# Score matmuls one key unit at a time, and output projections in four column groups

## The chip, the cores and the metric

The kernel runs on one core of one Trainium2 chip. A core has five engines with their own instruction streams: TensorE (PE in the profile, with its weight loads listed apart as PEld), VectorE (DVE), ScalarE (ACT), GpSimd (POOL) and SyncE (SP), which here does nothing but issue DMAs. Sixteen DMA engines move data between the device memory and the core's on-chip memory, SBUF. TensorE writes its results into PSUM, eight banks of 128 partitions by 512 fp32 values. The metric is the device time of one execution in microseconds, as a median of several runs.

## The reference

It is one decode step: a gated sum of an attention block (A) and a gated MLP (B), both fed by the same single row `x` of 1024 values.

```
g = sigmoid((x * gate_w).sum(-1))
q = x @ wq                              # 32 heads of 128
scores = q . k_cache * 128 ** -0.5      # 4 key heads, 65536 keys each; 8 query heads share one key head
p = softmax(scores); o = p . v_cache
a = o.reshape(4096) @ wo                # 4096 x 1024
z = gelu(x @ w_in)                      # 1024 x 3584, two halves z1 and z2
b = (z1 * (w_sp * layernorm(z2) + b_sp)) @ w_out    # 1792 x 1024
out = g * a + (1 - g) * b
```

Almost all of the data is the key and value cache: 2 x 4 x 65536 x 128 in bf16, 134 MB. The weights add 28 MB. Every byte is used once.

## The kernel before, in words

**The stream of loads.** All large inputs pass through a ring of five SBUF slots of 32 KB per partition (4 MB in all per slot). The list `stream` fixes the order: two loads of `wq`, then key pairs with the MLP's weights (`w_in`, `w_out`) in between, then key pairs and value pairs in turn, at the end value pairs alone, and last `wo` in six loads of 2, 2, 2, 1, 0.5 and 0.5 MB. A load of keys or values covers two units of 8192 rows, 4 MB. SP issues load number n (line 358) as soon as everything that reads load n - 5, the one before it in the same slot, is through. `use` and `done` place these issues in the program.

**A key unit.** One unit holds 64 keys on each of the 128 partitions. `k_piece` works on a quarter of it: DVE transposes 128 x 2048 bf16 as 32x32 blocks of fp32 words into a buffer `kt` (line 476), and TensorE multiplies it by the query (line 486). The query stands in `qpad`, a zero-padded buffer: for each of the four `fe` and each quarter j a 128 x 128 window of it is the stationary operand, and a 128 x 512 view of the transposed keys is the moving one. The 16 products of a unit add up in one PSUM bank, so that the scores of 8 heads and 16 groups of keys fill all 128 partitions. `score_piece` (line 499) then copies the bank to SBUF with a running maximum. In the kernel before, two units are treated together: in quarter j both are transposed, and each window of `qpad` is loaded once (the matmul at line 486) and used a second time by a matmul without a weight load (`again`, which the profile lists under line 247). A pair of units therefore takes two PSUM banks and two `kt` buffers at a time, and there are four of each (`SCB`, `NKTS`).

**Softmax and values.** After the eight units of a head, `max_piece` finds the maximum. ACT takes the exponentials (line 516), DVE transposes them (line 521), and TensorE multiplies them with the values (line 530): 16 matmuls of 512 columns, four at a time in four column groups of 32, into bank OB. Values lag keys by nine units. After the last unit of a head, `out_piece` normalises and brings the 1024 outputs of the head into `ovec` (lines 540 to 561).

**Output projections.** `wout_piece` forms the MLP's output row, and the loop at the end forms the attention's. Both take a column of 128 values as weights (one column wide) and stream rows of `w_out` or `wo`. In the kernel before, `project` writes one row of 1024 into partition 0 of two banks, 512 columns each, with one weight load for the two matmuls (lines 619 and 247). `keep` then moves this row to the four partitions 0, 32, 64 and 96 of `brow`, 256 values each: for the MLP by copies (line 638), for the first three parts of `wo` by additions (line 640). The last part of `wo` (heads 24 to 31, three loads) is done in another form (line 685): four column groups of 256 columns, one per quarter of the row, after a clearing of the bank (line 677). Line 691 adds `brow`, and line 694 writes the result.

**Order.** The kernel is a list of recorded operations. `Recorder.plan` derives semaphore waits from what each reads and writes, and each engine runs its own operations in recorded order.

Of the kernel before, what the change touches and what calls it, by code (L numbers as in the profile page):

```python
# [6 lines left out]
F32 = mybir.dt.float32  # L7
ACTF = mybir.ActivationFunctionType
ALU = mybir.AluOpType
# [128 lines left out]
def bass_gated_mix__gqa_block_cached__mixer_gmlp__decode_kernel(  # L138
# [19 lines left out]
    DO = A_wo.shape[1]  # L158
# [8 lines left out]
    NS = 5  # L167
    SLOT = 16384
    QP = 152
    NKTS = 4  # L170
    NSC = 8
    QW = DO // 4
    SCALE = 1.0 / math.sqrt(Dh)
    GELU_C = 0.044715
# [29 lines left out]
    def vw(base, off, dims, p0=0, np_=128):  # L204
        ps = base.ap[0][0]
        return bass.AP(tensor=base.tensor, offset=base.offset + off + p0 * ps,
                       ap=[[ps, np_]] + [list(d) for d in dims])
# [5 lines left out]
    qpad = [ab("QPAD", 4 * QP, 4 * QP * i) for i in range(2)]  # L213
# [3 lines left out]
    yb, ovec, orow, brow = ab("YB", FC), ab("OV", OC), ab("OROW", QW), af("BROW", QW)  # L217
# [14 lines left out]
    ktb = lambda i: ab("KT", 2048, (i % NKTS) * 2048)  # L232
# [3 lines left out]

    bank = [nc.alloc_psum_tensor("pb%d" % i, [128, 512], F32) for i in range(8)]
    FB, PTB, OB, MB = 0, 5, 6, 7
    WB0, WB1 = 0, 7
    SCB = [1, 2, 3, 4]  # L240
    pf = lambda i: bank[i][:, :]
    pbf = lambda i: bank[i][:, :].bitcast(BF16)

    def again(e, prev, out, rhs, start, stop):

        m = prev.ins
        return e.add_instruction(mybir.InstMatmult(  # L247
            start_tensor_calc=start, stop_tensor_calc=stop, tile_size=m.tile_size, tile_position=m.tile_position,
            bass_skip_group_check=True, ldweights=False, name=nc.get_next_instruction_name(), engine=e.engine,
            ins=[e.lower_ap(rhs), list(m.ins)[1]], outs=[e.lower_ap(out)]))  # L250

    R = Recorder()
    P = R.op

    def B(i):
        return ("bank", i)
# [7 lines left out]
        P("POOL", lambda e, i=i: e.memset(qpad[i], 0.0), w=[("qpad", i)])  # L264
    P("DVE", lambda e: e.memset(ones, 1.0), w=["ones"])
    P("DVE", lambda e: e.memset(oneb, 1.0), w=["oneb"])
    P("DVE", lambda e: e.memset(brow, 0.0), w=[("brow", q) for q in range(4)])
    P("DVE", lambda e: e.memset(pf(MB), 0.0), w=[B(MB)])
    P("DVE", lambda e: e.memset(pf(OB), 0.0), w=[B(OB)])
    P("DVE", lambda e: e.memset(pf(FB), 0.0), w=[B(FB)])  # L270
# [59 lines left out]
    for n in range(NU, total + NU + 1):  # L330
        k = n if n < total else None
# [9 lines left out]
    WO = [(0, 0, 8), (1, 0, 8), (2, 0, 8), (3, 0, 4), (3, 4, 6), (3, 6, 8)]  # L341
# [21 lines left out]
    def use(key):  # L363
        n, i = place[key]
        issue(n + 1)
        used.add(key)
        w = WIDTH[key[0]]
        return slot(n)[:, i * w:(i + 1) * w], ("slot", n % NS)

    def done(key):  # L370

        n = place[key][0]
        if key == stream[n][0][-1]:
            issue(n + NS + 1)
# [10 lines left out]
      r=["m32"], w=["sel"])  # L385
# [5 lines left out]
    for fe in range(4):  # L391
        P("DVE", lambda e, fe=fe: e.tensor_copy(vw(sele, 128 * fe, [[32, 4], [1, 32]]),
                                                vw(idb, 64 * (fe // 2) + fe % 2, [[0, 4], [2, 32]])),
          r=["idb"], w=[KSE])


    def f(e):
        for c in range(4):
            ins = e.transpose(pbf(PTB)[:, 2 * c:2 * c + 2], vw(xrow, c, [[4, 128]], 0, 2), idb[0:2, 0:2])
        return ins  # L400
    P("PE", f, r=[KX, "idb"], w=[B(PTB)])
    P("DVE", lambda e: e.tensor_copy(vw(xT, 0, [[4, 2], [1, 4]]), vw(pbf(PTB), 0, [[1, 2], [2, 4]])),
      w=["xT", B(PTB)])
    P("DVE", lambda e: e.tensor_copy(vw(xw, 1, [[3, KC]]), xT), r=["xT"], w=["xw"])
    P("PE", lambda e: e.matmul(pf(MB)[:, 0:2], oneb[0:1, :], wb[0:1, :], start=True, stop=True),  # L405
      r=["oneb", "wsp", "bsp"], w=[B(MB)])
# [6 lines left out]
      r=["ones", "gs"], w=[B(PTB)])  # L413
# [46 lines left out]
    def q_piece(g):  # L460
        for pb in range(4):
            P("DVE", lambda e, pb=pb: e.tensor_copy(vw(qpad[g % 2], 24 + 32 * pb, [[QP, 4], [1, 8]], 32 * pb, 32),
                                                    vw(qall, 8 * g, [[32, 4], [1, 8]], 32 * pb, 32)),
              r=["qall"], w=[("qpad", g % 2)])

    def k_piece(n, j):

        g, u = KV[n]
        if u == 0 and j == 0:
            q_piece(g)  # L470
        i = nbatch[0]
        nbatch[0] += 2
        sb = [SCB[n % 4], SCB[n % 4 + 1]]
        for m in range(2):
            sl, key = use(("k", n + m))
            P("DVE", lambda e, m=m, sl=sl: e.transpose(ktb(i + m).bitcast(F32),  # L476
                                                       sl[:, 2048 * j:2048 * (j + 1)].bitcast(F32)),
              r=[key], w=[("kt", (i + m) % NKTS)])

        def f(e):  # L480
            for fe in range(4):
                f2, ev = fe // 2, fe % 2
                o = QP * fe + 24 - 8 * j
                rhs = [vw(ktb(i + m), 64 * f2 + ev, [[128, 16], [2, 32]]) for m in range(2)]
                st, sp = j == 0 and fe == 0, j == 3 and fe == 3
                ins = e.matmul(pf(sb[0]), qpad[g % 2][:, o:o + 128], rhs[0], start=st, stop=sp)  # L486
                ins = again(e, ins, pf(sb[1]), rhs[1], st, sp)
            return ins
        P("PE", f, r=[("qpad", g % 2), ("kt", i % NKTS), ("kt", (i + 1) % NKTS)], w=[B(sb[0]), B(sb[1])])
        while pend:  # L490
            score_piece(pend.pop(0))
        if j == 3:
            done(("k", n + 1))
            pend.extend([n, n + 1])

    def score_piece(n):
        g, u = KV[n]
        sb = SCB[n % 4]
        P("DVE", lambda e: e.tensor_scalar(scs(n), pf(sb), 0.0, None, op0=ALU.add, op1=ALU.max,  # L499
                                           accum_out=maxc[:, n:n + 1]), w=[("sc", n % NSC), ("mx", n), B(sb)])  # L500
        if u == NU - 1:
            max_piece(g)
# [108 lines left out]
        P("DVE", lambda e: e.scalar_tensor_tensor(yb, z2[:, 0:FC], col(C_OMG), h1, op0=ALU.mult, op1=ALU.mult),  # L611
          r=["z2", "omg", "zg"], w=["yb"])

    def project(e, vec, sl, first, last):

        n = vec.shape[1]
        for c in range(n):
            st, sp = first and c == 0, last and c == n - 1
            ins = e.matmul(pf(WB0)[0:1, :], vec[:, c:c + 1], sl[:, DO * c:DO * c + 512], start=st, stop=sp,  # L619
                           skip_group_check=True)  # L620
            ins = again(e, ins, pf(WB1)[0:1, :], sl[:, DO * c + 512:DO * (c + 1)], st, sp)
        return ins

    def wout_piece(i):
        sl, key = use(("wout", i))
        P("PE", lambda e: project(e, yb[:, 7 * i:7 * (i + 1)], sl, i == 0, i == 1), r=["yb", key], w=[B(WB0), B(WB1)])
        done(("wout", i))
        if i == 1:
            keep(True)

    def keep(first):

        for q in range(4):
            src = pf((WB0, WB1)[q // 2])[0:1, QW * (q % 2):QW * (q % 2 + 1)]
            dst = brow[32 * q:32 * q + 1, :]
            k = [B((WB0, WB1)[q // 2])]
            if first:
                P("DVE", lambda e, dst=dst, src=src: e.tensor_copy(dst, src), w=[("brow", q)] + k)  # L638
            else:
                P("DVE", lambda e, dst=dst, src=src: e.tensor_tensor(dst, src, dst, ALU.add), r=[("brow", q)],  # L640
                  w=[("brow", q)] + k)


    started = set()
# [5 lines left out]

    for si, (k, v, aux) in enumerate(steps):
        nxt = steps[si + 1][1] if si + 1 < len(steps) else None
        while k is None and pend:
            score_piece(pend.pop(0))
        if v is not None and v not in started:
            start_exp(v)
        for j in range(4):
            if k is not None and j % 2 == 0:
                k_piece(k - k % 2, 2 * (k % 2) + j // 2)
            if j == 1 and v is not None:  # L660
                pt_piece(v)
            if j == 2 and nxt is not None:
                start_exp(nxt)
            if j == 3 and v is not None:
                pv_piece(v)
        for a in aux:
            (win_piece if a[0] == "win" else wout_piece)(a[1])


    for i in range(3):  # L670
        sl, key = use(("wo", i, 0))
        P("PE", lambda e, i=i, sl=sl: project(e, ovec[:, 8 * i:8 * (i + 1)], sl, i == 0, i == 2), r=[("ovec", i), key],
          w=[B(WB0), B(WB1)])
        done(("wo", i, 0))
    keep(False)
    FB = SCB[0]
    P("DVE", lambda e: e.memset(pf(FB), 0.0), w=[B(FB)])
    for i, c0, c1 in WO[3:]:
        sl, key = use(("wo", i, c0))

        def f(e, i=i, sl=sl, c0=c0, c1=c1):
            for c in range(c0, c1):
                for q in range(4):
                    o = DO * (c - c0) + QW * q
                    ins = e.matmul(pf(FB)[32 * q:32 * q + 1, 0:QW], ovec[:, 8 * i + c:8 * i + c + 1],  # L685
                                   sl[:, o:o + QW], start=(c == 0), stop=(c == 7),
                                   tile_position=(0, 32 * q), skip_group_check=True)
            return ins
        P("PE", f, r=[("ovec", i), key], w=[B(FB)])
        done(("wo", i, c0))  # L690
    P("DVE", lambda e: e.tensor_tensor(orow[0:97, :], pf(FB)[0:97, 0:QW], brow[0:97, :], ALU.add),
      r=[("brow", q) for q in range(4)], w=["orow", B(FB)])
    osrc = bass.AP(tensor=arena, offset=OFF["OROW"], ap=[[32 * NA, 4], [1, QW]])
    P("SP", lambda e: e.dma_start(out[0, 0].rearrange("(q n) -> q n", n=QW), osrc), r=["orow"], w=["out"], dma="out")

# [29 lines left out]
```

## Time and profile before

| what | value |
|---|---|
| median of 3 runs | 388.36 us (387.95 to 389.19) |
| the profiled execution's own time | 387.95 us |
| its span, first to last instruction | 386.2 us |
| mean granted TensorE clock | 0.80 of full |
| TensorE busy, matmuls | 237.5 us, 62% |
| TensorE busy, weight loads | 66.8 us, 17% |
| VectorE busy | 214.6 us, 56% |
| read from device memory | 162.01 MB, 420 GB/s over the span |

The span and the time differ by 1.75 us, which lie outside the instructions of the engines. Busy times of several engines overlap, so their sum says nothing; what counts is what the engine or the transfer that ended last was waiting for. "PEclk" or "granted clock" is the share of full TensorE speed. Window rows give, for a stretch of the span, each engine's busy time, the granted clock, the mean busy share of the sixteen DMA engines and their rate.

### The profile page before, as it was taken

To read this page: it belongs to the slowest core of one execution; us is meant where nothing else is said; L and a number is where in the kernel's file an instruction comes from. 1 tells how busy PE (TensorE), PEld (TensorE's weight loads), DVE (VectorE), ACT (ScalarE), POOL (GpSimd) and SP (SyncE) were. 2 spreads that over 40 slices of the span, in tenths; PEclk is the share of its full clock that TensorE was granted. 3 is DMA by queue.
4 is the path that set the end of the run, shared out by engine and by line. 5 is a ranking of instruction groups with operands and counts; after the bars stand their busy time and mean duration, and the time that the engine had idled before them with its cause. 6 is when DMAs were issued, how large, how long until landed. Compare 5 with 4: busy or idle time off the path is not lost.

```text
span 386.2 us, 3169 instructions
## 1 busy us (share of the span) xinstructions
PE 237.5 (62%) x1471; PEld 66.8 (17%) x1177; DVE 214.6 (56%) x338; ACT 30.0 (8%) x70; POOL 2.1 (1%) x9
## 2 busy tenths in 40 slices
PE   0443979477587766563668584735774838533394
PEld 0110444411111111011111110101110101211111
DVE  4115464397379983845389747554976557521102
ACT  1000000300002100000001000001010000320000
POOL 2000000000000000000000000000000000000000
PEclk9995869559968999695669786968896958665589
DMA  8999999999999999999999999999999999999992
GB/s 330 434 434 438 426 432 433 433 434 434 434 434 431 433 424 428 431 423 434 431 431 428 433 431 434 429 434 432 434 434 433 431 425 431 436 417 428 421 419 105
DMA packets 6226, 162.21 MB, mean 420 GB/s; under 512 B 700, under 2 KB 708, under 8 KB 964
## 3 DMA queue, kind: packets, MB, share of 16 engines
q1 hardware_dynamic: 6200, 162.01, 97.8%
q8 instruction: 10, 0.16, 0.2%
q14 instruction: 4, 0.03, 0.0%
q10 hardware_dynamic: 12, 0.00, 0.0%
HBM read 162.01 MB, written 0.00 MB: 420 GB/s over the span
## 4 chain that ended last, share of the span: by engine, by line
DMA 62%; PE 19%; DVE 17%; issue 1%; SPq 0%; DVEq 0%
DMA arena<-in_A_k_cache_dram 53%; DVE arena L476 13%; DMA arena<-in_A_v_cache_dram 10%; PE pb L247 7%; PE pb L486 5%; PE pb L619 2%; PE pb L530 2%; PE pb L572 2%; DVE arena L499 2%; DVE arena L521 1%; DVE arena L640 0%; DVE arena L638 0%; DVE arena L547 0%; PE pb L685 0%; PE pb L552 0%
## 5 line engine op out<-in xcount | busy, mean ns | idle before, releaser
L476 DVE STREAM_TRANSPOSE arena<-arena 128x1024 f32<-128x1024 f32 x128 | 149.1, 1212 | 67.2 <-DMA arena<-in_A_k_cache_dram 60.9
L486 PE MATMUL pb<-arena 128*128 128x512 bf16 x256 | 116.9, 456 | 95.5 <-DVE arena L476 88.8
L247 PE MATMUL pb<-arena 128*128 128x512 bf16 (+1 forms) x294 | 131.5, 447 | 0.0
L486 PEld LDWEIGHTS pb<-arena 128*128 128x128 bf16 x256 | 27.9, 109 | 208.1 <-DVE arena L476 123.0
L530 PE MATMUL pb<-arena 128*32 128x512 bf16 x512 | 39.7, 446 | 19.1 <-DMA arena<-in_A_v_cache_dram 16.6
L516 ACT ACTIVATE arena<-arena 128x512 bf16<-128x512 f32 x32 | 23.0, 719 | 245.0 <-DVE arena L521 153.3
L521 DVE STREAM_TRANSPOSE arena<-arena 128x512 bf16<-128x512 bf16 x32 | 22.1, 692 | 17.0 <-PE pb L530 17.0
L499 DVE TENSOR_SCALAR_CACHE_REDUCE arena<-pb 128x512 f32<-128x512 f32 x32 | 20.4, 672 | 2.5 <-PE pb L247 2.5
L530 PEld LDWEIGHTS pb<-arena 128*32 128x32 bf16 x512 | 13.0, 108 | 49.7 <-issue 41.8
L619 PE MATMUL pb<-arena 128*1 128x512 bf16 x38 | 15.4, 406 | 0.5 <-DVE arena L556 0.5
L572 PEld LDWEIGHTS pb<-arena 128*128 128x128 bf16 x224 | 13.8, 159 | 0.8 <-issue 0.7
L572 PE MATMUL pb<-arena 128*128 128x1 bf16 x224 | 13.7, 198 | 0.0
L544 DVE RECIPROCAL arena<-pb 128x1 f32<-128x1 f32 x4 | 0.7, 168 | 21.0 <-PE pb L542 21.0
L428 PE MATMUL pb<-arena 128*2 128x512 bf16 x64 | 7.2, 627 | 3.9 <-DMA arena<-in_A_wq_dram 3.9
L640 DVE TENSOR_TENSOR arena<-pb,arena 1x256 f32<-1x256 f32 x4 | 1.7, 415 | 12.2 <-PE pb L247 12.1
L435 DVE CAST arena<-pb 98x512 bf16<-98x512 f32 x1 | 0.7, 692 | 10.2 <-PE pb L428 10.2
L405 PE MATMUL pb<-arena 1*128 1x2 bf16 x1 | 0.2, 158 | 10.1 <-DMA arena<-in_B_b_sp_dram 10.1
L638 DVE COPY arena<-pb 1x256 f32<-1x256 f32 x4 | 1.7, 414 | 8.2 <-PE pb L247 8.1
L516 ACT ACTIVATION_READ_ACCUMULATOR arena<-arena 128x1 f32 x32 | 6.0, 186 | 0.0
L619 PEld LDWEIGHTS pb<-arena 128*1 128x1 bf16 x38 | 3.4, 88 | 15.1 <-issue 14.1
L583 DVE COPY arena<-pb 128x28 f32<-128x28 f32 x1 | 0.2, 187 | 8.7 <-PE pb L572 8.7
L552 PE MATMUL pb<-arena 128*128 128x128 bf16 x16 | 1.8, 244 | 5.2 <-DVE arena L547 5.2
(91 smaller groups left out, 49.7 us busy)
## 6 DMA issues: line engine op xcount, KB each, us to landing
arena<-in_A_k_cache_dram SPq DMA_DIRECT2D x16, 4096.0 KB, 28.9
arena<-in_A_v_cache_dram SPq DMA_DIRECT2D x16, 4096.0 KB, 34.0
arena<-in_A_wq_dram SPq DMA_DIRECT2D x2, 4096.0 KB, 16.9
arena<-in_B_w_in_dram SPq DMA_DIRECT2D x2, 3584.0 KB, 40.1
arena<-in_A_wo_dram SPq DMA_DIRECT2D x3, 2048.0 KB, 33.4
arena<-in_B_w_out_dram SPq DMA_DIRECT2D x1, 3584.0 KB, 34.9
arena<-in_A_wo_dram SPq DMA_DIRECT2D x1, 1024.0 KB, 23.1
arena<-in_A_wo_dram SPq DMA_DIRECT2D x2, 512.0 KB, 11.6
```

The costliest lines, as they stand in the source:

```text
L247: return e.add_instruction(mybir.InstMatmult(start_tensor_calc=start, stop_tensor_calc=stop, tile_size=m.tile_size, tile_position=m.tile_p ...
L428: ins = e.matmul(pf(OB)[32 * cg:32 * cg + 2, :], xw[:, 3 * c + 1 - s:3 * c + 3 - s], sl[:, WQ_N * k + 512 * (4 * s + cg):WQ_N * k + 512 * ...
L476: P("DVE", lambda e, m=m, sl=sl: e.transpose(ktb(i + m).bitcast(F32), sl[:, 2048 * j:2048 * (j + 1)].bitcast(F32)), r=[key], w=[("kt", (i ...
L486: ins = e.matmul(pf(sb[0]), qpad[g % 2][:, o:o + 128], rhs[0], start=st, stop=sp)
L499: P("DVE", lambda e: e.tensor_scalar(scs(n), pf(sb), 0.0, None, op0=ALU.add, op1=ALU.max, accum_out=maxc[:, n:n + 1]), w=[("sc", n % NSC), ...
L516: P("ACT", lambda e: e.activation(psb(n), scs(n), ACTF.Exp, bias=gcol(g, K_NB), scale=SCALE, accum_out=lp[:, n:n + 1]), r=[("sc", n % NSC) ...
L521: P("DVE", lambda e: e.transpose(ptsb(n), psb(n)), r=[("psb", n % 2)], w=[("ptsb", n % 2)])
L530: ins = e.matmul(pf(OB)[32 * cg:32 * (cg + 1), :], ptsb(n)[:, 32 * b:32 * (b + 1)], vw(sl, 128 * b, [[2048, 4], [1, 128]]), start=(u == 0 ...
L552: ins = e.matmul(pf(MB)[:, 0:128], sel[:, 128 * c:128 * (c + 1)], osc[:, 128 * c:128 * (c + 1)], start=(c == 0), stop=(c == 3))
L572: ins = e.matmul(pf(MB)[:, z:z + 1], vw(sl, c0, [[FC, 128]]), xT[:, 2 * i + k:2 * i + k + 1], start=(i == 0 and k == 0 and z == 0), stop=( ...
L619: ins = e.matmul(pf(WB0)[0:1, :], vec[:, c:c + 1], sl[:, DO * c:DO * c + 512], start=st, stop=sp, skip_group_check=True)
L638: P("DVE", lambda e, dst=dst, src=src: e.tensor_copy(dst, src), w=[("brow", q)] + k)
```

## The change

Three parts go together. Key units are worked one at a time again: per quarter one transpose and four matmuls, each with its own weight load; two PSUM banks for scores in place of four, three `kt` buffers in place of four, ten score buffers in place of eight. Both output projections use the form with four column groups of 256 columns, each matmul with its own one-column weight load: the MLP's into bank MB, from where a single ACT copy fills `brow`, and all of `wo` into bank FB, which is cleared once at the start. `project`, `keep`, `again` and the second clearing of FB go.

```diff
-    NKTS = 4
-    NSC = 8
+    NKTS = 3
+    NSC = 10
...
-    WB0, WB1 = 0, 7
-    SCB = [1, 2, 3, 4]
+    SCB = [3, 4]
...
     def k_piece(n, j):
...
+        sl, key = use(("k", n))
         i = nbatch[0]
-        nbatch[0] += 2
-        sb = [SCB[n % 4], SCB[n % 4 + 1]]
-        for m in range(2):
-            sl, key = use(("k", n + m))
-            P("DVE", lambda e, m=m, sl=sl: e.transpose(ktb(i + m).bitcast(F32),
-                                                       sl[:, 2048 * j:2048 * (j + 1)].bitcast(F32)),
-              r=[key], w=[("kt", (i + m) % NKTS)])
+        nbatch[0] += 1
+        P("DVE", lambda e: e.transpose(ktb(i).bitcast(F32), sl[:, 2048 * j:2048 * (j + 1)].bitcast(F32)),
+          r=[key], w=[("kt", i % NKTS)])
+        sb = SCB[n % 2]
...
-                rhs = [vw(ktb(i + m), 64 * f2 + ev, [[128, 16], [2, 32]]) for m in range(2)]
-                st, sp = j == 0 and fe == 0, j == 3 and fe == 3
-                ins = e.matmul(pf(sb[0]), qpad[g % 2][:, o:o + 128], rhs[0], start=st, stop=sp)
-                ins = again(e, ins, pf(sb[1]), rhs[1], st, sp)
+                ins = e.matmul(pf(sb), qpad[g % 2][:, o:o + 128], vw(ktb(i), 64 * f2 + ev, [[128, 16], [2, 32]]),
+                               start=(j == 0 and fe == 0), stop=(j == 3 and fe == 3))
...
-        while pend:
+        if pend:
             score_piece(pend.pop(0))
         if j == 3:
-            done(("k", n + 1))
-            pend.extend([n, n + 1])
+            done(("k", n))
+            pend.append(n)
...
     def wout_piece(i):
         sl, key = use(("wout", i))
-        P("PE", lambda e: project(e, yb[:, 7 * i:7 * (i + 1)], sl, i == 0, i == 1), r=["yb", key], w=[B(WB0), B(WB1)])
+        def f(e):
+            for c in range(7):
+                for q in range(4):
+                    ins = e.matmul(pf(MB)[32 * q:32 * q + 1, 0:QW], yb[:, 7 * i + c:7 * i + c + 1],
+                                   sl[:, DO * c + QW * q:DO * c + QW * (q + 1)],
+                                   start=(i == 0 and c == 0), stop=(i == 1 and c == 6), tile_position=(0, 32 * q),
+                                   skip_group_check=True)
+            return ins
+        P("PE", f, r=["yb", key], w=[B(MB)])
         done(("wout", i))
         if i == 1:
-            keep(True)
+            P("ACT", lambda e: e.activation(brow[0:97, :], pf(MB)[0:97, 0:QW], ACTF.Copy), w=["brow", B(MB)])
...
-            if k is not None and j % 2 == 0:
-                k_piece(k - k % 2, 2 * (k % 2) + j // 2)
+            if k is not None:
+                k_piece(k, j)
...
-    for i in range(3):
-        sl, key = use(("wo", i, 0))
-        P("PE", lambda e, i=i, sl=sl: project(e, ovec[:, 8 * i:8 * (i + 1)], sl, i == 0, i == 2), r=[("ovec", i), key],
-          w=[B(WB0), B(WB1)])
-        done(("wo", i, 0))
-    keep(False)
-    FB = SCB[0]
-    P("DVE", lambda e: e.memset(pf(FB), 0.0), w=[B(FB)])
-    for i, c0, c1 in WO[3:]:
+    for i, c0, c1 in WO:
...
-                                   sl[:, o:o + QW], start=(c == 0), stop=(c == 7),
+                                   sl[:, o:o + QW], start=(i == 0 and c == 0), stop=(i == 3 and c == 7),
```

## The prediction

> **What bounds the kernel now.** I read the page's slices first, then its groups, then the time from issue to landing of the loads, and then the end of the chain and of the windows. The slices (40 of 9.65 us; busy tenths, DMA share, rate):
>
> ```profile
> PEclk9995869559968999695669786968896958665589
> DMA  8999999999999999999999999999999999999992
> GB/s 330 434 434 438 426 432 433 433 434 434 434 434 431 433 424 428 431 423 434 431 431 428 433 431 434 429 434 432 434 434 433 431 425 431 436 417 428 421 419 105
> ```
>
> The DMA engines are full from the second slice to the last but one, at some 432 GB/s, so 4.19 MB (4096 KB) take 9.7 us, and a key pair with its value pair 19.4 us. TensorE and VectorE could gain or lose much and nothing would move, as long as the queue is not empty. Whether it ever is follows from how long before its landing a load is issued. For keys, then for values:
>
> ```profile
> DMA to landing us min/median/max: 23.5/28.9/49.2
> ```
>
> ```profile
> DMA to landing us min/median/max: 23.6/34.0/38.1
> ```
>
> The shortest is 23.5 us. A load needs 9.7 us itself, and by the trace's landing records the sixteen engines finish one load up to 3.4 us apart late in the run. So at least 23.5 - 9.7 - 3.4 = 10.4 us of other loads are queued whenever one is issued: the reserve in the middle. What is left is the end. The last stretch of the chain, start, duration and what, and windows of half a microsecond (PE, PEld, DVE, ACT, POOL busy, clock, DMA share, GB/s):
>
> ```profile
> 376.58 0.38 PE pb L619
> ...
> 379.98 0.23 PE pb L247
> ...
> 380.23 0.41 DVE arena L640
> ...
> 381.51 0.42 DVE arena L640
> 381.93 0.10 issue
> 382.03 0.50 DVE pb L677
> ...
> 382.57 1.07 PE pb L685 x31
> ...
> 383.67 0.42 DVE arena L691
> ```
>
> ```profile
> 378.00:378.50 0.50, 0.50 (x4) 0.09 (x1) 0.00 (x0) 0.00 (x0) 0.00 (x0) 1.00 0.61 246
> 380.50:381.00 0.50, 0.00 (x0) 0.00 (x0) 0.49 (x2) 0.00 (x0) 0.00 (x0) 1.00 0.14 57
> 381.00:381.50 0.50, 0.00 (x0) 0.00 (x0) 0.48 (x2) 0.00 (x0) 0.00 (x0) 1.00 0.00 0
> ```
>
> The third part of `wo` is there at 376.5; then come its 16 matmuls, four additions, a clearing, and only then the matmuls of the last part. Yet DMA has nearly stopped by 381.0. The last load was issued at 373.15 and the shortest issue-to-landing among the `wo` loads is 8.3 us, so the last byte is there at 381.45. From there to the end of the span (386.16) pass 4.7 us.
>
> **The change, part by part.**
>
> *Key units.* The products are the same: 512 matmuls of 128 x 512, 128 transposes, 32 score copies. Weight loads go from 256 to 512. The groups price one:
>
> ```profile
> L486 PEld LDWEIGHTS pb<-arena 128*128 128x128 bf16 x256 | 27.9, 109 | 208.1 <-DVE arena L476 123.0 <-issue 71.1 <-DVE arena L540 6.9
> L476 DVE STREAM_TRANSPOSE arena<-arena 128x1024 f32<-128x1024 f32 x128 | 149.1, 1212 | 67.2 <-DMA arena<-in_A_k_cache_dram 60.9 <-PE pb L247 6.3
> ```
>
> So 256 x 0.109 = 27.9 us more load time. The timeline shows where a load lies:
>
> ```profile
> 36.08 0.63 PE L247 MATMUL pb<-arena 128*128 128x512 bf16 x1
> 36.08 0.14 PEld L486 LDWEIGHTS pb<-arena 128*128 128x128 bf16 x1 [0.71 <-issue]
> 36.50 0.63 PE L486 MATMUL pb<-arena 128*128 128x512 bf16 x1
> 36.93 0.63 PE L247 MATMUL pb<-arena 128*128 128x512 bf16 x1
> ```
>
> The load starts with the matmul before its own, and starts are 0.42 and 0.43 apart with and without one: it is hidden. I take 0 for TensorE's pace. Between 0 and 27.9 us of TensorE time nothing reaches the end, because the reserve covers it: a pair at half clock in the run before, keys landed at 176.16, let SP issue the next loads at 191.14, 15.0 us later, in a period of 19.4; 16 exposed loads of 0.14 would make 17.2. The Trainium skill speaks against this part. Its page "TensorE: Matmul & The Clock Gate", Part 3, "The mechanism", says that a weight load overlaps matmuls in flight only where it goes to other row groups; these loads fill all of them, so by the rule the 27.9 us would be added to TensorE's work, where the rows above make it 0. By either, the sum at the end is the same unless the reserve goes.
>
> VectorE's work is unchanged: two units are 8 x 1.21 + 2 x 0.67 + 2 x 0.69 = 12.4 us of 19.4. With three `kt` buffers the fourth transpose waits for the matmuls of the first; at half clock those are 4 x 0.43 = 1.7 us against 1.2 per transpose, so TensorE sets the pace as now. Score copies wait for one unit's last matmuls; behind them on VectorE stand the next transposes, and TensorE has 16 value matmuls (1.0 to 1.8 us) to do meanwhile. A key slot is freed by the eighth transpose, as before. I count 0; what is late next is the value slot, with 10.4 us in hand.
>
> *MLP projection.* 28 matmul pairs (some 6 us, at 96 to 102 us in the chain) become 112 matmuls in column groups. The nearest row is line 685: 32 in 1.04 us, so 3.6 us. Four copies at line 638 (1.7 us) become one ACT copy of 97 x 256 (below the 0.72 of a 128 x 512 ACTIVATE; at most 1.28 more for a table load). ACT's first exponential came at 115 us. Hidden behind the load stream: 0 either way.
>
> *The end.* Three projections of 16 matmuls (3.5 us each) become three of 32 in 1.04 us at full clock, twice that at half. The third starts when its load lands (376.55) and ends by 378.7, before the fourth's first load (1 MB, some 2.4 us after) has landed. The four additions (1.70), the clearing (0.48) and their gaps go. SP's last issue, queued behind the release of the first `wo` slot, moves from 373.15 to some 369.5; it still stands behind what is queued, so landing stays at 381.45. After it come the 8 matmuls of the last load. At full clock that is two rounds of 0.107 and a drain of 0.18 (32 took 1.04), 0.4 us; at half clock two of 0.213 (half the columns of a 0.43 matmul) and 0.2, 0.6 us. With short bursts between landings, the clock at 348 to 364 us was 0.50, so I take 0.6; both ends are kept. Sum: 381.45 + 0.05 (wake, as at 376.58) + 0.6 + 0.06 + 2.49 (line 691's start to the span's end, as now) = 384.65, against 386.16: **1.5 us less**, 1.7 at full clock. The profiled execution would take 387.95 - 1.5 = 386.4; the median of the runs stands 0.41 above that one, so 386.85, and I say **386.8**.
>
> *Instruction fetch.* TensorE's instructions grow by 256 for keys, 70 for the MLP and 120 for `wo`: 446 on 1471 + 1177. The DMA view lists 10 instruction packets of 16 KB on one queue, 265 of these instructions each, so 1.7 packets more. In the landing records the spread over the sixteen engines grew from 0.57 us at the first loads to 3.4 at the end, in steps of up to 1.3 near such packets. If one more falls on the engine that is last anyway, the last landing is 1.3 later; if the draw is luckier, as much earlier. I take 0, since two more over sixteen engines mostly miss the last one. "Runtime: NRT & Kernel Launch", "Instruction fetch mechanics", calls the cost of a block mostly hidden, which would leave the 1.5 whole; the spread in the landing records says it isn't always.
>
> **The rivals.**
>
> *One more packet on the last engine.* For: the growth above. Against: few packets. 386.8 + 1.3 = 388.1, no change; two more: 389.4, on the edge of slower. One fewer: 385.5.
>
> *The end is not shortened,* because TensorE is behind or the last landing is later than I read it: 388.4. Against: 32 matmuls in 1.04 us, with 4.9 us between 2 MB landings.
>
> *Slower: TensorE at half clock with exposed loads empties the queue,* at the key and value pairs from 110 to 320 us. Price: each microsecond that a pair takes beyond 19.4 comes off the 10.4 and then off the end. It decides from 4.4 us more per pair (15.0 to 19.4), 0.28 per added load, twice the 0.14 seen. At 7.4 more the reserve lasts 3.5 of 12 pairs, and the other 8.5 cost 3 each: 386.8 + 25 = 412. Against: a TensorE that is never idle got full clock in the run before (0.50 at 36 to 40 us, 1.00 by 44).
>
> **How the numbers follow.** Runs of this kernel lie 0.3% apart, and 0.3% (1.17 us) is what I count as a change. Forecast 0.64, three quarters of it over 0.3% (0.48), as 1.5 is only a little above 1.17; one packet fewer 0.07, faster; one more or no gain 0.12, same; two more 0.07, half same, half slower; queue empty 0.10, slower. Faster 0.55, same 0.31, slower 0.14. The range, 385.4 to 389.5, runs from one packet fewer (385.5) to two more (389.4) and leaves out the empty queue.
>
> **What the profile after would show.** Rate still 432 GB/s to the last slice but one; shortest issue-to-landing of keys and values over 13 us; line 486's matmuls 0.43 or 0.22 apart though each has a load; after the last landing a short burst at line 685's successor, one addition, and the end 3.2 us later. I am wrong if a slice in the middle falls below 420 GB/s, or the last landing is later than 382.

## The result, and the profile after

The changed kernel takes 386.63 us in the median of six runs (386.58 to 386.90), against 388.60 us (387.95 to 389.19) for six runs of the kernel before: a ratio of 0.995, with a 95% interval of 0.9938 to 0.9963. That is a gain of 2.0 us in the medians. The forecast was 386.8. The two profiled executions are 387.95 and 386.75 us, their spans 386.16 and 384.87: 1.3 us apart.

Where the time went shows at the end of the chain of the kernel after (start, duration, what):

```profile
368.21 1.83 PE pb L650 x32
370.04 0.01 issue
370.06 11.62 DMA arena<-in_A_wo_dram
381.68 0.04 issue
381.73 0.62 PE pb L650 x6
382.35 0.02 issue
382.37 0.42 DVE arena L656
```

Before, the chain ran from the landing of the last values at 361.84 to the end through TensorE and VectorE, and through no transfer of `wo`. Now it runs through one, and what follows the last landing at 381.68 is a burst of 0.62 us, one addition and the output. The timeline of the same stretch shows that TensorE now waits for each load of `wo` in turn, the bracket being the idle time before and what ended it:

```profile
376.80 1.87 PE L650 MATMUL pb<-arena 128*1 128x256 bf16 x32 [3.05 <-DMA arena<-in_A_wo_dram]
...
379.38 1.71 PE L650 MATMUL pb<-arena 128*1 128x256 bf16 x24 [0.71 <-DMA arena<-in_A_wo_dram]
...
381.73 0.60 PE L650 MATMUL pb<-arena 128*1 128x256 bf16 x8 [0.64 <-DMA arena<-in_A_wo_dram]
382.37 0.42 DVE L656 TENSOR_TENSOR arena<-pb,arena 97x256 bf16<-97x256 f32 x1 [13.41 <-PE pb L650]
```

In the middle nothing moved. From the page's slices:

```profile
DMA  8999999999999999999999999999999999999994
GB/s 331 436 433 440 430 424 437 429 435 433 427 433 426 427 433 429 433 432 436 433 429 436 424 429 436 429 431 430 433 433 431 433 430 429 434 433 422 421 418 169
```

The stream is as full as before. The last slice moved 169 GB/s where it had moved 105, only because the shorter span's slices are shorter and the last begins 1.3 us earlier.

The page's groups price the key units (busy, mean ns of one, idle before and its releaser):

```profile
L472 PE MATMUL pb<-arena 128*128 128x512 bf16 x512 | 160.0, 457 | 93.6 <-DVE arena L464 91.7
L472 PEld LDWEIGHTS pb<-arena 128*128 128x128 bf16 x512 | 46.7, 109 | 201.3 <-DVE arena L464 144.9
```

Twice the loads, at the same 109 ns each. The timeline of the first key unit, at half clock, shows their distance:

```profile
34.41 6.74 PE L472 MATMUL pb<-arena 128*128 128x512 bf16 x19
35.26 0.14 PEld L472 LDWEIGHTS pb<-arena 128*128 128x128 bf16 x1 [0.28 <-DVE arena L464]
35.69 0.14 PEld L472 LDWEIGHTS pb<-arena 128*128 128x128 bf16 x1 [0.28 <-issue]
36.12 0.14 PEld L472 LDWEIGHTS pb<-arena 128*128 128x128 bf16 x1 [0.28 <-issue]
36.54 0.14 PEld L472 LDWEIGHTS pb<-arena 128*128 128x128 bf16 x1 [0.28 <-issue]
```

They are 0.43 us apart, the pace that matmuls without a load of their own had before. At full clock, too, the starts of neighbouring key matmuls lie 0.22 us apart (median) in both kernels. The added loads cost TensorE's pace nothing.

What I had not forecast is in the loads' time from issue to landing, for keys and then for values:

```profile
DMA to landing us min/median/max: 27.7/30.9/49.3
```

```profile
DMA to landing us min/median/max: 28.9/36.4/37.5
```

The shortest rose from 23.5 and 23.6 us. Loads are issued earlier: the reserve in the queue grew by 4 us, where I had counted on no change.

### The profile page after: what moved, and what is told of

It reads as the page before. It is cut to its first block, busy times and chain, and to the rows that moved or that the text cites. A ratio compares the mean times of both kernels' runs of the same rounds, so it can differ in the third digit from the quotient of the medians.

```text
span 384.9 us, 3607 instructions
## 1 busy us (share of the span) xinstructions
PE 233.6 (61%) x1547; PEld 86.2 (22%) x1547; DVE 211.6 (55%) x329; ACT 30.6 (8%) x71; POOL 2.1 (1%) x9
## 4 chain that ended last, share of the span: by engine, by line
DMA 71%; PE 16%; DVE 11%; issue 0%; SPq 0%
DMA arena<-in_A_k_cache_dram 59%; PE pb L472 11%; DMA arena<-in_A_v_cache_dram 10%; DVE arena L464 9%; DMA arena<-in_A_wo_dram 3%; PE pb L516 2%; PE pb L558 2%; DVE arena L485 1%; PE pb L650 1%; DVE arena L507 0%; DVE arena L533 0%; PE pb L538 0%; PE pb L528 0%; SPq L349 0%; PE pb L495 0%
## 5 line engine op out<-in xcount | busy, mean ns | idle before, releaser
L472 PE MATMUL pb<-arena 128*128 128x512 bf16 x512 | 160.0, 457 | 93.6 <-DVE arena L464 91.7
L464 DVE STREAM_TRANSPOSE arena<-arena 128x1024 f32<-128x1024 f32 x128 | 151.4, 1217 | 75.3 <-DMA arena<-in_A_k_cache_dram 75.0
L472 PEld LDWEIGHTS pb<-arena 128*128 128x128 bf16 x512 | 46.7, 109 | 201.3 <-DVE arena L464 144.9
L485 DVE TENSOR_SCALAR_CACHE_REDUCE arena<-pb 128x512 f32<-128x512 f32 x32 | 21.6, 674 | 8.1 <-PE pb L472 7.9
L558 PEld LDWEIGHTS pb<-arena 128*128 128x128 bf16 x224 | 13.8, 161 | 0.4
L650 PE MATMUL pb<-arena 128*1 128x256 bf16 x128 | 7.8, 410 | 6.3 <-DMA arena<-in_A_wo_dram 6.3
```

What stands on the lines that cost most here:

```text
L464: P("DVE", lambda e: e.transpose(ktb(i).bitcast(F32), sl[:, 2048 * j:2048 * (j + 1)].bitcast(F32)), r=[key], w=[("kt", i % NKTS)])
L472: ins = e.matmul(pf(sb), qpad[g % 2][:, o:o + 128], vw(ktb(i), 64 * f2 + ev, [[128, 16], [2, 32]]), start=(j == 0 and fe == 0), stop=(j == ...
L558: ins = e.matmul(pf(MB)[:, z:z + 1], vw(sl, c0, [[FC, 128]]), xT[:, 2 * i + k:2 * i + k + 1], start=(i == 0 and k == 0 and z == 0), stop=( ...
```

## The experiments

The theory: the stream of loads bounds the kernel, so only the end can move the time, and there the last part of `wo` no longer waits behind other work. Rival one: the key units free their slots earlier, and this is the gain. Rival two: the number of TensorE's instructions, which are themselves fetched by DMA, decides the last landing.

### Only the end of the new kernel

In the kernel before, all of `wo` goes through the column groups; key pairs and the MLP projection stay.

```diff
-    for i in range(3):
-        ...project(e, ovec[:, 8 * i:8 * (i + 1)], sl, i == 0, i == 2)...
-    keep(False)
-    FB = SCB[0]
-    P("DVE", lambda e: e.memset(pf(FB), 0.0), w=[B(FB)])
-    for i, c0, c1 in WO[3:]:
+    for i, c0, c1 in WO:
```

> The paired key units and the MLP projection of the kernel before, with only the end changed: all of wo in four column groups, no additions and no second clearing. Theory (the whole gain sits at the end): 1.5 to 2 us less than before, 386.6 to 387.1, and 3.2 us from the last landing to the end of the span. Rival (the gain comes from key slots that come free earlier): as before, 388.6. Rival (instruction fetch decides the last landing): with 120 instructions more than before in place of 446, a last landing earlier than the 381.7 of after, and a time below 386.6.

Measured: 386.62 us (386.41 to 386.96), ratio 0.9953 (0.9934 to 0.9971). That is the whole gain, and rival one falls. The last landing is at 381.81, and 3.2 us follow it. Rival two's earlier landing did not come, though this kernel fetched 11 instruction packets where after fetched 12.

### Only the key units

```diff
-    NKTS = 4
-    NSC = 8
+    NKTS = 3
+    NSC = 10
...
-    SCB = [1, 2, 3, 4]
+    SCB = [3, 4]
...
-                k_piece(k - k % 2, 2 * (k % 2) + j // 2)
+                k_piece(k, j)
```

> Only the key units changed: one at a time, a weight load for each matmul; both projections as before. Theory of the end: no change, 388.6 within 0.3%, last landing at 381.5 give or take 0.4. Rival (keys): the gain of 1.5 to 2 us is here, 386.6 to 387.1. Either way I expect the shortest issue-to-landing of keys to rise from 23.5 to some 27.7 us, as in after.

Measured: 388.19 us, ratio 0.9998 (0.9981 to 1.0014): no change, with the last landing at 381.52, as expected. The shortest issue-to-landing of keys is 25.1 us, not the 27.7 I expected, and of values 23.3, so the larger reserve is not from the key units alone.

### Only the MLP projection

```diff
-        P("PE", lambda e: project(e, yb[:, 7 * i:7 * (i + 1)], sl, i == 0, i == 1), r=["yb", key], w=[B(WB0), B(WB1)])
+        P("PE", f, r=["yb", key], w=[B(MB)])    # f: four column groups, as in the change
...
-            keep(True)
+            P("ACT", lambda e: e.activation(brow[0:97, :], pf(MB)[0:97, 0:QW], ACTF.Copy), ...)
```

> Only the MLP projection changed: column groups into one bank and one ACT copy into brow; key units and the end as before. All theories: no change, 388.6 within 0.3%; at 96 to 102 us some 3 us less of TensorE work that nothing waits for.

Measured: 389.02 us, ratio 1.0011 (0.9993 to 1.0030): no change. But the shortest issue-to-landing of values rose from 23.6 to 26.6. The reason stands in the timeline of VectorE in the kernel before:

```profile
93.02 1.20 DVE L476 STREAM_TRANSPOSE arena<-arena 128x1024 f32<-128x1024 f32 x1
102.37 1.70 DVE L638 COPY arena<-pb 1x256 f32<-1x256 f32 x4 [8.14 <-PE pb L247]
104.08 2.37 DVE L476 STREAM_TRANSPOSE arena<-arena 128x1024 f32<-128x1024 f32 x2
```

`keep`'s copies stood in VectorE's queue ahead of key transposes that were ready to run, and waited 8.1 us for the MLP projection. With the copy on ACT, VectorE goes on, and the loads that follow are issued earlier: the third value load at 112.4 in place of 123.1 us. This cost the kernel before nothing, as the queue was never empty.

### The clearing of the bank, moved earlier

This is the kernel before, with one statement moved.

```diff
+    FB = SCB[0]
+    P("DVE", lambda e: e.memset(pf(FB), 0.0), w=[B(FB)])
     for i in range(3):
         sl, key = use(("wo", i, 0))
...
     keep(False)
-    FB = SCB[0]
-    P("DVE", lambda e: e.memset(pf(FB), 0.0), w=[B(FB)])
```

> The kernel before with the second clearing of the bank moved ahead of the wo projections, where VectorE is idle; nothing else changed. Theory (the end is a serial chain from the last matmul of project on): the clearing's 0.48 us and its gap of 0.1 come off, 0.5 to 0.6 us less, about 388.0. If the last landing already bounds it, less than 0.2.

Measured: 386.55 us, ratio 0.9955 (0.9940 to 0.9970). I expected 0.5 to 0.6 us, and it is all of the gain. My reading of the chain was too serial. The last stretch of its chain:

```profile
372.11 9.57 DMA arena<-in_A_wo_dram
381.68 0.04 issue
381.73 0.42 PE pb L685 x8
...
382.24 0.42 DVE arena L691
```

And the timeline of the same stretch:

```profile
380.03 1.03 PE L685 MATMUL pb<-arena 128*1 128x256 bf16 x18
380.44 1.70 DVE L640 TENSOR_TENSOR arena<-pb,arena 1x256 f32<-1x256 f32 x4 [11.12 <-PE pb L247]
381.73 0.39 PE L685 MATMUL pb<-arena 128*1 128x256 bf16 x8 [0.67 <-DMA arena<-in_A_wo_dram]
```

The matmuls of the last part never needed the four additions; only the final addition does. They needed the cleared bank, and the clearing stood behind the additions in VectorE's queue, which in turn waited for the third part. Once the clearing is early, the matmuls run as their loads land, and the additions (380.44 to 382.14) lie beside them. They are through just when the last burst is, so there was no room to spare.

### The late clearing, put back into the new kernel

The mirror image: after, but the first three parts go into one bank, then an addition and the clearing of a second bank follow on VectorE, and the last part goes into that bank.

```diff
-    for i, c0, c1 in WO:
+    part(WO[:3], FB, 0, 2)     # the same loop, into bank FB
+    P("DVE", lambda e: e.tensor_tensor(brow[0:97, :], pf(FB)[0:97, 0:QW], brow[0:97, :], ALU.add), ...)
+    P("DVE", lambda e: e.memset(pf(1), 0.0), w=[B(1)])
+    part(WO[3:], 1, 3, 3)
```

> The kernel after, with the late clearing of before put back: the first three parts of wo in column groups into one bank, then an addition into brow and the clearing of a second bank on VectorE, and only then the matmuls of the last part, into that second bank. Theory (what counts is that the last part's matmuls can start before the last landing): the third part ends at 378.7, the addition and the clearing by 379.8, so the last landing at 381.7 still ends the wait, and the time is that of after, 386.6. Rival (a late clearing costs time in either form): 0.5 to 1 us more, 387.1 to 387.6.

Measured: 386.66 us (386.44 to 386.79), ratio 0.9939 (0.9916 to 0.9963), the time of after. The third part now ends early enough that the late clearing is through before the last landing, by the timeline:

```profile
376.59 1.88 PE L651 MATMUL pb<-arena 128*1 128x256 bf16 x32 [3.20 <-DMA arena<-in_A_wo_dram]
378.52 0.42 DVE L659 TENSOR_TENSOR arena<-pb,arena 97x256 f32<-97x256 f32 x1 [10.38 <-PE pb L651]
379.05 0.48 DVE L661 MEMSET pb<- 128x512 f32 x1
379.59 1.45 PE L651 MATMUL pb<-arena 128*1 128x256 bf16 x24 [1.12 <-DVE pb L661]
381.52 0.60 PE L651 MATMUL pb<-arena 128*1 128x256 bf16 x8 [0.49 <-DMA arena<-in_A_wo_dram]
```

So either remedy is enough by itself: the faster form of the third part (with one addition in place of four), or the earlier clearing. Each lets the wait end with the landing, and neither adds to the other.

### Four ring slots, before and after

```diff
-    NS = 5
+    NS = 4
```

> The kernel before with a ring of four slots in place of five: loads are issued 9.7 us later, so the reserve of 10.4 us by the shortest issue-to-landing is nearly gone. Theory (the order of the key units matters only for the reserve): the queue runs dry in places, DMA falls below 420 GB/s in slices between 110 and 320 us, and the time rises by some us, 390 to 400. Rival (the stream is bound by something else than issue): no change, 388.6.

> The kernel after with four slots. In after the shortest issue-to-landing is 27.7 us, 4.2 more than before, so by the theory the reserve is still some 4 us and the time stays within 1 us of after, 386.6 to 387.6, well below the same edit on before. If exposed weight loads slowed TensorE, it would lose as much as before with four slots, or more.

Measured: before with four slots 389.52 us (387.81 to 392.83), ratio 1.0030 (1.0000 to 1.0060), just below the 390 to 400 that I had expected, and the interval reaches down to no change; after with four slots 386.80 us (386.65 to 386.93), ratio 0.9954 (0.9940 to 0.9969), 0.2 above after with five. Slices 13 to 15 of the kernel before with four slots (421, 396 and 414 GB/s, 116 to 146 us) show the queue running dry (by the landing records, the engine that is done first lands loads 9.7 us apart, and here once 10.4):

```profile
GB/s 334 431 434 433 454 428 425 431 434 431 431 431 421 396 414 431 431 427 434 431 431 429 431 431 431 429 434 432 428 434 429 431 439 431 433 431 421 424 368 68
```

In this execution, 391.10 us long, the last values land 1.1 us later than in before (362.94 against 361.84), and the span is 3.1 us longer. The other 2 us lie behind the stream: TensorE, on the chain without a wait for `wo`, had more of its work at half clock (0.50 from 362 to 374), and its last 32 matmuls took 1.9 us against 1.04. Its last load of `wo` was issued at 379.10, after some engines had run out of work at 378.60. That cost nothing here, as the load was there at 383.31 and the matmuls that read it waited for the clearing:

```profile
384.36 0.50 DVE pb L677
384.86 0.04 issue
384.90 1.91 PE pb L685 x32
```

After with four slots never ran dry. What the change did to the middle is a gain in reserve that five slots hide; with four it is worth some 1 us by these two profiles.

### More instructions

After each quarter of a key unit, eight matmuls of one column into an unused bank are added to after, each with its weight load.

```diff
+            for _ in range(8):
+                ins = e.matmul(pf(1)[0:1, 0:1], oneb[:, 0:1], oneb[:, 1:2], start=True, stop=True)
```

> The kernel after with eight matmuls of 128 x 1 by 1 into an unused bank after each quarter of a key unit: 1024 matmuls and 1024 weight loads that compute nothing, 2048 instructions, some 8 instruction packets more than the 12 of after. Theory (each packet delays one of the sixteen DMA engines by 1.1 to 1.3 us): the spread of the landings grows by one or two steps at the most loaded engine, the last landing moves from 381.7 to 383 or 384, and the time rises by 1 to 2.5 us, 387.6 to 389.2. Rival (fetch is hidden): 386.6, spread 3.6 as in after. TensorE's extra work, 1 to 2 us per unit of 9.7, is covered by the reserve under both.

Measured: 388.13 us (387.91 to 388.29), 1.5 us above after. The DMA view lists 20 instruction packets on that queue, where after has 12:

```profile
q8 instruction: 20, 0.33, 0.3%
```

By the landing records, the sixteen engines finish the last load 4.9 us apart in place of 3.6; the first of them is done at 378.20, as in after (378.10). Seven engines are done by 378.81 (in after, seven by 378.98), the other nine between 381.22 and 383.14 (in after, 379.80 to 381.68). The chain ends in the same way, 1.46 us later:

```profile
371.53 11.61 DMA arena<-in_A_wo_dram
383.14 0.04 issue
383.18 0.63 PE pb L652 x8
383.81 0.02 issue
383.83 0.42 DVE arena L658
```

The shortest issue-to-landing of keys is 25.7 us, so TensorE's extra work did not empty the queue. Nor did a late issue move the end: it would have held up the first seven engines too, and the last values, ahead of all of `wo`, had landed 1.46 us later already (363.51 against 362.05). What is left is fetching.

### Fewer instructions

The early clearing again, with 29 of the 224 products with `w_in`; 195 matmuls and their weight loads of the MLP's first projection are left out.

```diff
-                for z in range(2 * FC):
+                for z in range(2 * FC if i == 0 and k == 0 else 1 if i == 3 and k == 1 else 0):
```

> The kernel with the early clearing and 29 of the 224 products with w_in (it leaves 195 matmuls and 195 weight loads of the MLP's first projection out; every load of data stays): 390 instructions of TensorE less, 8 or 9 packets of 16 KB in place of 10. Theory of fetch: if a packet less falls on an engine that is among the last, the last landing comes up to 1.3 us earlier than the 381.7 of the early clearing, 385.3 to 386.5 us; if not, no change, 386.55. A later landing would speak against the theory.

Measured: 386.29 us (386.12 to 386.43), ratio 0.9926 (0.9901 to 0.9952). Nine packets in place of ten, a spread of 3.0 us in place of 3.4, the last landing at 381.26 in place of 381.68, and 0.26 us less than the early clearing alone. The direction is that of the theory, but the size is within the spread of one kernel's executions (386.41 to 386.96 for the first experiment), so by itself this run proves little.

## Why the prediction was right

**The bound.** Right: the stream of loads, full from the second slice to the last but one, before and after, and an end of 4.7 us after the last landing.

**Key units at 0.** Right in the sum (no change in the run with this part alone) and in the pace (0.43 us per matmul, each with its load). The rule in "TensorE: Matmul & The Clock Gate", Part 3, "The mechanism", that a weight load overlaps matmuls in flight only in other row groups, does not hold here as it stands: the loads fill all row groups and lie under the matmul before. The same section also names a load into a background weight buffer as one that runs ahead; no run here shows which buffer a load goes to. "What is late next is the value slot" held for this part alone (shortest issue-to-landing 23.3 us for values, 25.1 for keys). With the whole change both came free earlier (28.9 and 27.7).

**MLP projection at 0.** Right in the sum. The counts were not: 14 columns make 28 matmuls before and 56 after, not 28 pairs and 112, and their busy time after is 1.7 us, not 3.6. And the copies' wait of 8.1 us on VectorE, with key transposes queued behind, I had passed over; it was hidden by the reserve of 10.4 us. With four slots the kernel before runs dry in the stretch that follows it; that this wait is the cause there was not tried by itself.

**The end at 1.5.** The working held term by term: last landing 381.45 forecast and 381.68 found, burst 0.6 and 0.60 (at half clock, as taken), start of the final addition to the end 2.49 and 2.50. Hence 384.65 and 384.87 for the span. The landing is the 0.2 us. A smaller reading failed: it lists additions and clearing alike as what must go. The additions were on the chain only because the clearing stood behind them, as the early clearing showed. And it sets the third part's start by its landing alone; TensorE itself had only just finished the second part, at 376.57.

**The medians.** That 386.8 lies so close to 386.63 is in part luck, as two errors cancel. The profiled execution took 386.75 where 386.4 was forecast, and the median stands 0.12 below it where it was taken to stand 0.41 above. The medians moved by 2.0 and not by 1.5, as the profiled execution of before is one of its fastest. What sets its executions apart was not tried, but the traces suggest TensorE's clock: from 367.82 to 380.21 its chain is TensorE's work without a break, and its 32 last matmuls took 1.04 us at full clock. In the profiled execution of the kernel with only the MLP changed, which ends in the same way, they took 1.89 at half clock, and its span is 387.1:

```profile
382.14 0.50 DVE pb L687
382.64 0.04 issue
382.68 1.89 PE pb L695 x32
384.57 0.02 issue
384.60 0.42 DVE arena L701
```

Runs of before lie around 388.2 and around 389.0, which fits these two. A few at 390.2 were not profiled, and I leave them open. After, with 8 matmuls behind the last landing, spreads over 0.3 us only.

**Instruction fetch.** The mechanism I took as a rival exists: 446 more instructions made two more packets (12 for 10), with a last landing 0.2 later, too little to be told from chance; 2048 more moved it by another 1.46. "Runtime: NRT & Kernel Launch", "Instruction fetch mechanics", calls this cost mostly hidden; where the loads bound the kernel to its end it is not. **The slower rival** (exposed loads empty the queue) saw nothing: the queue became deeper.

## What to carry to other kernels

When a stream of loads bounds a kernel, look first at what follows the last landing, and ask of each wait there what it really needs: here one clearing stood behind unrelated work in an in-order queue, and moving one statement gave as much as the whole change. A chain shows an order, not a need; an operation on it may be there only because another stands behind it. Reserve in the queue hides other losses, and taking a slot from the ring can show them.

## What the hardware showed that I had not expected

The landing records fit a simple picture: every 16 KB packet of TensorE instructions takes a turn on one of the sixteen DMA engines that carry the data. With 10 packets in the run before, the engines that began 0.6 us apart ended 3.4 apart; with after's 12 it was 3.6, and with 20 it was 4.9, and the end came 1.5 us later than in after. In a kernel that ends with its last byte, an instruction has a price even when TensorE is idle for a third of the time: about 0.7 ns each in the run with 2048 more (1.46 us / 2048), in steps, as it counts only where a packet falls on the engine that is last. Seven engines end within 0.9 us of the first with 10, 12 and 20 packets alike (378.11 to 378.85 in before), so it looks as if the other nine take them all. Which engine takes which packet the records don't tell, so whether the packets could be kept off the last one stays open.
